# Slots by rank of token count: 576 or 600 per expert, with weights loaded from register addresses

## The chip, the cores and the metric

The kernel runs on one core of a Trainium2 chip. A core has five engines with queues of their own: TensorE (PE in the profile, with its weight loads as PEld), VectorE (DVE), ScalarE (ACT), GpSimd (POOL), and SyncE (SP), which here mostly issues DMA transfers. The metric is device time in microseconds (us); lower is better. The profile is of one execution and names source lines as L123.

## The reference

Attention with a threshold is followed by a mixture of experts that routes every token by a hash of its id.

```python
# q, k, v: (8, 8, 576, 64) float32
scores = np.matmul(q, k.transpose(0, 1, 3, 2)) / np.sqrt(64)
thresh = np.max(scores, axis=-1, keepdims=True) - tau
scores = np.where(scores >= thresh, scores, -1e9)
attn = np.exp(scores - np.max(scores, axis=-1, keepdims=True))
attn = attn / (np.sum(attn, axis=-1, keepdims=True) + 1e-09)
x = np.matmul(attn, v)      # laid out as (4608 tokens, 512)
expert_idx = token_ids * np.int64(2654435761) % np.int64(8)
for e in range(8):          # w1: (8, 512, 1024), w2: (8, 1024, 512)
    mask = expert_idx == e
    out[mask] = np.maximum(x[mask] @ w1[e], 0.0) @ w2[e]
```

All data is float32. The seed of the inputs is fixed, so the number of tokens of each expert is known: 598, 596, 571, 565, 599, 533, 570 and 576 for experts 0 to 7.

## The kernel before

**Attention** takes about 455 us and loops over 32 pairs of heads. A pair `p` has `NS = 5` steps `n`: one with the last 64 queries of both heads and four with 128 queries. `score` (L222) forms scores on TensorE, `negate` (L233) moves them from PSUM with their row extreme on VectorE, `expo` (L247) is the exponential on ScalarE. GpSimd forms the threshold `thr` (L240), and `mask` (L258) on VectorE multiplies weights by the threshold test and sums them. `turn_w` transposes on TensorE (L269), `put_wT` copies (L290), `av_part` multiplies by v (L300), and `put_xm` (L339) normalises and stores 128 columns of the attention result to the DRAM tensor `x_scratch` (L345, L350). The order of everything is written out by hand in the loop over `n` (L656 to L751) and each queue keeps it. In step `n`, masks belong to step `n - 1` and transposes to step `n - 2`. SP loads pairs two ahead. GpSimd also scales k (`scale_k`, L202).

**Routing** is a generator, `route()` (L353). Each `next(pieces)` issues a few small operations on `[128, 8]`, `[128, 36]` or `[128, 288]` elements, up to the next `yield`. It is called at two steps of a pair (L670 and L721) until `placed`. The route counts tokens per expert, finds each token's rank in its expert and then its slot. The slots of expert `e` are a region of `SL = 608`, laid out as 32 columns of 19; the first 24 columns take 19 tokens and the last eight take 18, which makes `CAP = 600`. Tokens past `CAP` go to overflow tiles of 128 slots. Then `scatters()` (L492) writes token numbers to slot tables in DRAM (`slot_scratch`), one indirect DMA of GpSimd per step, and SP reads the tables back (L506, L510) as indices for gathers and scatters of rows.

**The move to the experts.** `load_w1` and `load_w2` for experts 0 and 1 are issued on SP in pairs 20, 22, 24 and 26. From pair 26 on GpSimd gathers columns of `x_scratch` for expert 0 (`fetch_0`, L119, L113). `early_xT` transposes them, and `early_h` (L587) does three quarters of expert 0's first layer ahead of the last gather. `late_h` (L604) adds the last quarter.

**Experts** go in the order 0 to 7, one at a time, from about 490 us. Both layers use a scheme of seven products on half matrices (`seven`, L846) instead of eight. The two halves of the token dimension have `CH = CAP // 2 = 300` columns; the matmuls are at L859. VectorE forms sums of half matrices (L791, L794), ScalarE copies and applies the relu (L869, L866). The last expert's second layer works on two halves of 240 (`CHL`), and a separate last tile (L908) does the rest. `put_out` (L915) transposes output rows on TensorE (L927), copies them (L937, L939) and scatters them to their places with GpSimd (L943). `turn_x` (L959) transposes the next expert's rows on VectorE and moves quarters by SP's DMA (L971). During expert `e`, SP loads the weights of `e + 2`. A loop over overflow tiles follows; the number of its turns is read to registers by `values_load` at L1039. With the counts above it has none.

Each weight load names its expert when the program is built:

```python
def load_w1(e):
    w1_sb = w_pool.tile([P, CO, F], FP32, name="w1_sb")
    nc.sync.dma_start(out=w1_sb[:], in_=w1[e].rearrange("(c p) f -> p c f", p=P))
```

## Time and profile before

| | |
|---|---|
| time, median of 3 runs | 948.47 us (948.05 to 948.58) |
| profiled execution, its own time | 950.67 us |
| its span, first to last instruction | 949.0 us |
| TensorE busy, share | 933.1 us, 98% |
| VectorE busy, share | 734.1 us, 77% |
| ScalarE busy, share | 478.1 us, 50% |
| GpSimd busy, share | 306.1 us, 32% |
| granted TensorE clock | 0.998 |

Busy shares are averages over two stages with different limits. Matmul ends are modelled, so the distance between starts says more than the length of one. A float32 matmul appears as two records. In a row of the timeline, "x16" is the number of instructions merged, and a bracket at the end gives the idle time before the row and what ended it. In a table of windows, each engine has its busy time and in parentheses the number of its instructions; then come the granted clock, the share of the DMA engines' time and GB/s. In groups by line, the numbers after the bar are busy time, mean ns of one, and idle time before. Rows with three times (as 477/477/477) give the shortest, median and longest duration in ns.

### The profile page before, as it was taken

The numbers are of one execution on the slowest core, as the hardware profiler recorded it, in microseconds if no ns is written. First come the engines' busy times: TensorE is split into PE (matmuls) and PEld (weight loads), VectorE is DVE, ScalarE is ACT, GpSimd is POOL, SyncE is SP. The second block draws the span as 40 slices with busy tenths as digits, with TensorE's granted clock in tenths as the row PEclk, the third lists the DMA queues.
The fourth block names the chain that finished last, engine by engine and source line by source line (L and its number), as shares of the span: only waits on it lengthen the run. The fifth ranks groups of instructions, "written<-read, shape, count | busy, mean of one in ns | idle before, by whom it ended". The sixth has DMA issues, their size and how long they took to land.

```text
span 949.0 us, 21042 instructions
## 1 busy us (share of the span) xinstructions
PE 933.1 (98%) x7779; PEld 645.1 (68%) x7779; DVE 734.1 (77%) x1638; ACT 478.1 (50%) x778; POOL 306.1 (32%) x413
## 2 busy tenths in 40 slices
PE   8999999999999999999999999999999999999996
PEld 5666666666666666666677777777777777777785
DVE  7999999999999999999457755756557566575541
ACT  6988888888898888888320211202112021120310
POOL 4233233237767633565034310403003030110202
PEclk9999999999999999999999999999999999999999
DMA  7355456446447866841017435254442445311101
GB/s 174 90 142 133 106 133 144 104 125 138 103 91 213 204 164 143 202 107 39 26 31 216 159 93 175 89 156 158 109 158 89 142 159 140 139 46 34 50 1 51
DMA packets 113511, 113.31 MB, mean 119 GB/s; under 512 B 31183, under 2 KB 88015, under 8 KB 113409
## 3 DMA queue, kind: packets, MB, share of 16 engines
q1 hardware_dynamic: 105168, 92.84, 36.5%
q0 software_dynamic: 7808, 18.91, 6.6%
q8 instruction: 63, 1.03, 0.5%
q14 instruction: 40, 0.32, 0.1%
q10 hardware_dynamic: 432, 0.21, 0.1%
HBM read 81.99 MB, written 21.72 MB: 109 GB/s over the span
## 4 chain that ended last, share of the span: by engine, by line
PE 58%; issue 31%; DVE 5%; POOL 2%; DMA 2%; ACT 1%; SPq 0%; POOLq 0%; DVEq 0%; ACTq 0%
PE av L300 16%; PE sc L222 14%; PE bank L859 13%; PE tr L269 10%; PE sc L587 3%; DVE w L258 2%; PE av L269 1%; DVE ns L233 1%; POOL out_dram L943 1%; DMA out_dram<-o_sb,gidx 1%; DVE xq L963 1%; ACT w L247 1%; POOL xg L113 1%; PE xT_ps L604 0%; PE sc L604 0%
## 5 line engine op out<-in xcount | busy, mean ns | idle before, releaser
L247 ACT ACTIVATE w<-ns,nmx 128x576 f32<-128x576 f32 x288 | 220.4, 776 | 34.9 <-DVE ns L233 34.7
L258 DVE SCALAR_TENSOR_TENSOR w<-ns,thr,w 128x576 f32<-128x576 f32 x288 | 226.0, 816 | 1.3 <-POOL thr L240 1.3
L233 DVE TENSOR_SCALAR_CACHE_REDUCE ns<-sc 128x576 f32<-128x576 f32 x288 | 205.2, 744 | 3.9 <-PE sc L222 3.1
L222 PE MATMUL sc<-k_sb,q 64*128 64x288 f32 (+1 forms) x1280 | 179.8, 426 | 0.8 <-DVE ns L233 0.4
L269 PEld LDWEIGHTS tr<-ident,w 64*128 64x128 f32 x2624 | 106.4, 138 | 88.0 <-ACT wT_b L290 26.0
L240 POOL TENSOR_SCALAR thr<-nmx,drop 128x2 f32<-128x2 f32 (+1 forms) x160 | 103.2, 645 | 182.9 <-DVE ns L233 172.2
L943 POOL DMA_INDIRECT out_dram<-o_sb,gidx x39 | 47.6, 1220 | 292.4 <-ACT o_sb L939 277.5
L269 PE MATMUL tr<-ident,w 64*128 64x64 f32 x2624 | 138.7, 230 | 2.6 <-ACT wT_a L290 2.0
L869 ACT COPY p<-bank 128x600 f32<-128x600 f32 (+1 forms) x22 | 14.4, 654 | 201.4 <-PE bank L859 200.6
L222 PEld LDWEIGHTS sc<-k_sb,q 64*128 64x128 f32 (+1 forms) x1280 | 93.0, 179 | 24.0 <-DVE ns L233 10.6
L300 PE MATMUL av<-wT_a,v 128*64 128x320 f32 (+1 forms) x704 | 100.4, 418 | 0.0
L866 ACT ACTIVATE h<-h 128x600 f32<-128x600 f32 x56 | 39.4, 703 | 119.5 <-DVE h L794 119.0
L859 PE MATMUL bank<-h,w_sb 128*128 128x300 f32 (+1 forms) x384 | 97.3, 410 | 0.9 <-DVE h L609 0.9
L290 ACT COPY wT_a<-tr 128x512 f32<-128x512 f32 (+1 forms) x128 | 81.7, 638 | 19.8 <-PE tr L269 19.5
L859 PE MATMUL bank<-xT,w_sb 128*128 128x300 f32 x336 | 89.4, 416 | 0.0
L859 PEld LDWEIGHTS bank<-h,w_sb 128*128 128x128 f32 x384 | 72.9, 190 | 22.9 <-DVE h L609 1.3
L290 ACT COPY wT_b<-tr 128x512 f32<-128x512 f32 (+1 forms) x128 | 81.2, 635 | 5.0 <-PE tr L269 2.6
L300 PE MATMUL av<-wT_b,v 128*64 128x256 f32 x640 | 83.2, 389 | 0.0
L859 PEld LDWEIGHTS bank<-xT,w_sb 128*128 128x128 f32 x336 | 63.8, 190 | 21.0
L859 PE MATMUL bank<-h_s,w_s 128*128 128x300 f32 (+1 forms) x256 | 64.3, 410 | 0.0
L300 PEld LDWEIGHTS av<-wT_a,v 128*64 128x64 f32 x704 | 43.7, 136 | 28.6
L859 PE MATMUL bank<-x_s,w_s 128*128 128x300 f32 x224 | 59.6, 419 | 0.0
(147 smaller groups left out, 1106.7 us busy)
## 6 DMA issues: line engine op xcount, KB each, us to landing
w_sb<-in_moe_w_dram SPq DMA_DIRECT2D x16, 2048.0 KB
q<-in_q_dram SPq DMA_DIRECT2D x62, 288.0 KB
v<-in_v_dram SPq DMA_DIRECT2D x32, 256.0 KB
x_scratch<-xm SPq DMA_DIRECT2D x32, 256.0 KB
xT<-xq SPq DMA_DIRECT2D x84, 80.0 KB
k_sb<-in_k_dram SPq DMA_DIRECT2D x31, 144.0 KB
k_sb<-in_k_dram SPq DMA_DIRECT2D x32, 112.0 KB
x_scratch<-xg SPq DMA_DIRECT2D x9, 256.0 KB
```

Of the source, the lines that this page charges most:

```text
L222: nc.tensor.matmul(sc[out_rows, i, 0:S2], lhsT=q_sb[rows, h, q0:q1], rhs=k_sb[rows, h], start=True, stop=True)
L233: nc.vector.tensor_scalar(out=ns[:].rearrange("p (i s) -> p i s", i=2), in0=sc[:, :, 0:S2], scalar1=-1.0, scalar2=None, op0=ALU.mult, op1= ...
L240: nc.gpsimd.tensor_scalar(out=thr[:, 0:j + 1], in0=stats[n][0][:, 0:j + 1], scalar1=drop[:], scalar2=None, op0=ALU.add)
L247: nc.scalar.activation(w, nss[n, j][:], AF.Exp, bias=stats[n][0][:, j:j + 1], scale=-1.0)
L258: nc.vector.scalar_tensor_tensor(out=w, in0=nss.pop((n, j))[:], scalar=stats[n][1][:, j:j + 1], in1=w, op0=ALU.is_le, op1=ALU.mult, accum_ ...
L269: nc.tensor.transpose(dst[:, r, 64 * c:64 * c + 64], src[rows, c0:c0 + P], ident[rows, rows])
L290: nc.scalar.copy(dst, tr[:, :, 0:64 * n_c].rearrange("p r (c q) -> p r c q", c=n_c))
L300: nc.tensor.matmul(av[64 * j:64 * j + 64, g, c0:c1], lhsT=v_sb[:, c, 64 * j:64 * j + 64], rhs=wT[g][:, i, c0:c1], start=(c == 0), stop=stop)
L587: nc.tensor.matmul(h_ps[:, i, 0:CH], lhsT=w1_sb[:, co, fo * P:fo * P + P], rhs=xT_0[:, co, i * CH:i * CH + CH], start=(co == 0), stop=(co ...
L859: nc.tensor.matmul(ps[:, i, 0:width], lhsT=x[:, c, c0:c0 + P], rhs=y[:, c], start=c == 0, stop=c == n_k - 1)
L866: nc.scalar.activation(c, c, AF.Relu)
L943: inst = nc.gpsimd.indirect_dma_start(out=out[:, :], out_offset=bass.IndirectOffsetOnAxis(ap=idx, axis=0), in_=o_sb, in_offset=None, bound ...
```

## The change

Experts are taken in the order of their token counts. The route compares a key, count times 8 plus the expert's number, among all experts: `pos` is an expert's place in the order and `order` its inverse. Places 0 to 4 have `LOW = 576` slots (32 columns of 18), places 5 to 7 have 600 as before. Regions still start every 608 slots, now by place and not by expert. The rank is packed with the place (from bit 19) and the first overflow tile (six bits from bit 13). Several steps of the route go from VectorE to GpSimd. Three more calls of the route are added, at step 2 of pairs 9, 11 and 13.

`order_i` holds the order as integers. Each of the 16 weight loads on SP first reads its expert from there to a register (`expert_at`) and takes the DRAM address from it. All half widths of an expert in places 0 to 4 become 288, and its fifth tile of output rows has 64 rows, not 88. The expert in the last place keeps its 240-column halves.

```diff
@@ -59,14 +59,20 @@
+    N_LOW = 5
+    LOW = SL - 32
+    caps = [LOW] * N_LOW + [CAP] * (E - N_LOW)
...
-    TROWS = [P] * (KT - 1) + [CAP - FIRST[-1]]
-    CH = CAP // 2
...
+    def t_rows(e, kt):
+        return min(P, caps[e] - FIRST[kt])
...
-    assert all((N - (m - 1) * (CAP + 1) - CAP + P - 1) // P + m - 1 <= NOV
-               for m in range(1, E + 1) if m * (CAP + 1) <= N)
+    assert all((N - (m - 1) * (LOW + 1) - LOW + P - 1) // P + m - 1 <= NOV
+               for m in range(1, E + 1) if m * (LOW + 1) <= N)
+    assert all((r * 3641) >> 16 == r // (NB - 1) for r in range(N))
@@ -118,14 +125,21 @@
+    def expert_at(e):
+        return nc.values_load(order_i[0:1, e:e + 1], engines=[mybir.EngineType.SP],
+                              min_val=0, max_val=E - 1)
...
-        nc.sync.dma_start(out=w1_sb[:], in_=w1[e].rearrange("(c p) f -> p c f", p=P))
+        nc.sync.dma_start(out=w1_sb[:],
+                          in_=w1[bass.ds(expert_at(e), 1)].rearrange("o (c p) f -> p (o c) f", p=P))
...
-        nc.sync.dma_start(out=w2_sb[:], in_=w2[e].rearrange("(c p) d -> p c d", p=P))
+        nc.sync.dma_start(out=w2_sb[:],
+                          in_=w2[bass.ds(expert_at(e), 1)].rearrange("o (c p) d -> p (o c) d", p=P))
@@ -414,7 +435,27 @@
-            nc.vector.tensor_scalar(out=ot_i[:], in0=cnt[:, E:2 * E], scalar1=float(P - 1 - CAP),
+            nc.vector.scalar_tensor_tensor(out=key[:], in0=cnt[:, E:2 * E], scalar=float(E),
+                                           in1=iota_f[:, 0:E], op0=ALU.mult, op1=ALU.add)
+            nc.vector.tensor_tensor(out=pairs[:], in0=key[:, None, :].to_broadcast([P, E, E]),
+                                    in1=key[:, :, None].to_broadcast([P, E, E]), op=ALU.is_lt)
+            yield
+            nc.vector.reduce_sum(pos[:], pairs[:], axis=AX.X)
+            nc.gpsimd.tensor_scalar(out=big_e[:], in0=pos[:], scalar1=float(N_LOW),
+                                    scalar2=None, op0=ALU.is_ge)
+            nc.vector.tensor_tensor(out=pairs[:], in0=pos[:, None, :].to_broadcast([P, E, E]),
+                                    in1=iota_f[:, 0:E, None].to_broadcast([P, E, E]),
+                                    op=ALU.is_equal)
+            nc.gpsimd.tensor_tensor(out=pairs[:], in0=pairs[:],
+                                    in1=iota_f[:, None, 0:E].to_broadcast([P, E, E]),
+                                    op=ALU.mult)
+            yield
+            nc.vector.scalar_tensor_tensor(out=key[:], in0=big_e[:], scalar=float(LOW - CAP),
+                                           in1=cnt[:, E:2 * E], op0=ALU.mult, op1=ALU.add)
+            nc.vector.reduce_sum(order[:], pairs[:], axis=AX.X)
+            nc.gpsimd.tensor_copy(order_i[:], order[:])
+            yield
+            nc.vector.tensor_scalar(out=ot_i[:], in0=key[:], scalar1=float(P - 1 - LOW),
@@ -429,6 +470,8 @@
+            nc.vector.scalar_tensor_tensor(out=base[:], in0=pos[:], scalar=float(1 << 19),
+                                           in1=base[:], op0=ALU.mult, op1=ALU.add)
@@ -443,29 +486,40 @@
-            nc.vector.tensor_scalar(out=rank_i[:, 2], in0=rank_i[:, 0], scalar1=13, scalar2=None,
+            nc.vector.tensor_scalar(out=rank_i[:, 2], in0=rank_i[:, 0], scalar1=13, scalar2=63,
+                                    op0=ALU.logical_shift_right, op1=ALU.bitwise_and)
+            nc.vector.tensor_scalar(out=rank_i[:, 3], in0=rank_i[:, 0], scalar1=19, scalar2=None,
...
-            yield
-            nc.vector.tensor_copy(rank[:], rank_i[:, 1])
-            nc.vector.tensor_scalar(out=rank_f[:], in0=rank[:], scalar1=float(-1 - FULL), scalar2=0.0,
+            nc.gpsimd.tensor_copy(rank[:], rank_i[:, 1])
+            nc.gpsimd.tensor_copy(place[:], rank_i[:, 3])
+            nc.gpsimd.tensor_scalar(out=big[:], in0=place[:], scalar1=float(N_LOW),
+                                    scalar2=None, op0=ALU.is_ge)
+            nc.gpsimd.tensor_copy(ovt[:], rank_i[:, 2])
+            yield
+            nc.vector.scalar_tensor_tensor(out=rank_f[:], in0=big[:], scalar=float(-FULL),
+                                           in1=rank[:], op0=ALU.mult, op1=ALU.add)
+            nc.gpsimd.tensor_scalar(out=rank_f[:], in0=rank_f[:], scalar1=-1.0, scalar2=0.0,
...
-            yield
-            nc.vector.tensor_copy(ovt[:], rank_i[:, 2])
-            nc.vector.tensor_scalar(out=rank_i[:, 0], in0=rank_f[:], scalar1=57.0, scalar2=None,
+            nc.gpsimd.tensor_scalar(out=ovt[:], in0=ovt[:], scalar1=float(P),
+                                    scalar2=float(E * SL - LOW), op0=ALU.mult, op1=ALU.add)
+            yield
+            nc.vector.tensor_scalar(out=rank_i[:, 0], in0=rank_f[:], scalar1=3641.0, scalar2=None,
...
-            nc.vector.tensor_scalar(out=rank_i[:, 0], in0=rank_i[:, 0], scalar1=10, scalar2=None,
+            nc.vector.tensor_scalar(out=rank_i[:, 0], in0=rank_i[:, 0], scalar1=16, scalar2=None,
...
-            nc.vector.tensor_scalar(out=ovt[:], in0=ovt[:], scalar1=float(P),
-                                    scalar2=float(E * SL - CAP), op0=ALU.mult, op1=ALU.add)
-            nc.vector.scalar_tensor_tensor(out=first[:], in0=eidf[:], scalar=float(SL),
+            nc.vector.scalar_tensor_tensor(out=first[:], in0=place[:], scalar=float(SL),
...
-            yield
-            nc.vector.tensor_tensor(out=ovt[:], in0=ovt[:], in1=first[:], op=ALU.subtract)
-            nc.vector.scalar_tensor_tensor(out=ovt[:], in0=rank[:], scalar=float(CAP),
+            nc.vector.scalar_tensor_tensor(out=rank_f[:], in0=big[:], scalar=float(LOW - CAP),
+                                           in1=rank[:], op0=ALU.mult, op1=ALU.add)
+            nc.vector.scalar_tensor_tensor(out=ovt[:], in0=big[:], scalar=float(LOW - CAP),
+                                           in1=ovt[:], op0=ALU.mult, op1=ALU.add)
+            yield
+            nc.gpsimd.tensor_tensor(out=ovt[:], in0=ovt[:], in1=first[:], op=ALU.subtract)
+            yield
+            nc.vector.scalar_tensor_tensor(out=ovt[:], in0=rank_f[:], scalar=float(LOW),
...
-            yield
-            nc.vector.tensor_tensor(out=first[:], in0=first[:], in1=rank[:], op=ALU.add)
+            nc.gpsimd.tensor_tensor(out=first[:], in0=first[:], in1=rank[:], op=ALU.add)
@@ -584,15 +642,16 @@
-                        nc.tensor.matmul(h_ps[:, i, 0:CH], lhsT=w1_sb[:, co, fo * P:fo * P + P],
-                                         rhs=xT_0[:, co, i * CH:i * CH + CH],
+                        nc.tensor.matmul(h_ps[:, i, 0:CH0], lhsT=w1_sb[:, co, fo * P:fo * P + P],
+                                         rhs=xT_0[:, co, i * CH0:i * CH0 + CH0],
...
-                                h_0[:, fo].rearrange("p (i t) -> p i t", i=2), h_ps[:, :, 0:CH])
+                                h_0[:, fo, 0:caps[0]].rearrange("p (i t) -> p i t", i=2),
+                                h_ps[:, :, 0:CH0])
@@ -667,7 +726,7 @@
-                if s == 3 and p > 0 and not placed:
+                if (s == 3 and p > 0 or s == 2 and p in (9, 11, 13)) and not placed:
@@ -810,8 +870,10 @@
-        def x_blocks(x):
-            return [x[:, C2 * j:C2 * j + C2, CH * k:CH * k + CH] for j in range(2) for k in range(2)]
+        def x_blocks(e):
+            x, half = xT_bufs[e % 2], caps[e] // 2
+            return [x[:, C2 * j:C2 * j + C2, half * k:half * k + half]
+                    for j in range(2) for k in range(2)]
@@ -821,7 +883,7 @@
-            return CH if e < E - 1 else CHL
+            return caps[e] // 2 if e < E - 1 else CHL
```

The same widths replace `CH` and `TROWS` in the early and late parts of layer 1, in `sums_x`, `layer1`, `put_out` and `turn_x`.

## The prediction

> **What bounds the kernel now.** I read the busy totals and the forty slices first, then the table of windows, then the timelines of single engines where a window raised a question.
>
> ```profile
> PE 933.1 (98%) x7779; PEld 645.1 (68%) x7779; DVE 734.1 (77%) x1638; ACT 478.1 (50%) x778; POOL 306.1 (32%) x413
> ...
> DVE  7999999999999999999457755756557566575541
> ```
>
> A busy PE of 98% says little alone, because the ends of matmuls are modelled. The second line divides the kernel: VectorE is full for some 19 of 40 slices (attention, to about 455 us) and about six tenths busy after (experts). Two windows, one head pair of attention and one expert, give the bound of each stage. The columns are length, then PE, PEld, DVE, ACT and POOL busy time.
>
> ```profile
> 257.13:271.02 13.89, 13.89 (x178) 8.81 (x174) 13.84 (x39) 12.29 (x21) 9.92 (x13) 1.00 0.49 108
> ```
>
> ```profile
> 559.90:618.50 58.60, 58.35 (x265) 43.66 (x264) 36.91 (x47) 10.21 (x16) 11.17 (x10) 1.00 0.43 134
> ```
>
> A pair lasts 13.89 us and VectorE works 13.84 of them: attention is bound by VectorE, with TensorE close behind. An expert lasts 58.6 us, TensorE works 58.35, VectorE 36.91, ScalarE 10.21: the expert stage is bound by TensorE alone, and what is taken from its matmuls is taken from the end. Weight loads (PEld, 190 ns each) lie beneath the matmuls. In the PE timeline of the last two experts:
>
> ```profile
> 866.72 4.20 PE L859 MATMUL bank<-h_s,w_sb 128*128 128x300 f32 x16
> 870.75 4.20 PE L859 MATMUL bank<-h,w_sb 128*128 128x300 f32 x16
> ...
> 922.37 3.40 PE L859 MATMUL bank<-h_s,w_sb 128*128 128x240 f32 x16
> 925.61 3.40 PE L859 MATMUL bank<-h,w_sb 128*128 128x240 f32 x16
> ```
>
> From start to start, 16 records of 300 columns take 4.03 us (252 ns each) and 16 of 240 columns take 3.24 us (202.5 ns). Sixty columns are worth 49 to 50 ns, so the price is 0.83 ns a column with no fixed part to be seen, and 288 columns, between the two, should cost 10.0 ns less than 300.
>
> **Part 1, narrower matmuls (gain).** Experts in places 0 to 4 go from two halves of 300 to two of 288. Each layer of an expert has 112 records (7 products x 2 x 4 matmuls in the second layer, each seen as two records). Place 0 has 96 early and 32 late records of layer 1 and 112 of layer 2, which is 240. Places 1 to 4 have 224 each, 896. In sum 1136 x 10.0 ns = **11.4 us**. Places 5 to 7 keep 300, and the last layer keeps its 240. The early records hide the last gathers: these are issued from 475.38 to 482.67 us, land 2.5 to 3.0 us after their start for the last two, so by about 485, and TensorE comes to their transposes at 486.99. With 64 early records behind the last `xm`, 0.64 us of this 2 us cover goes, and none is paid. VectorE and ScalarE get shorter too (24 elements of a 600-element add), under TensorE and worth nothing. The counts (533, 565, 570, 571, 576 and 596, 598, 599) fit 576 and 600, so the overflow loop stays at zero turns in both kernels.
>
> **Part 2, an old wait grows (loss).** In layer 1 TensorE reaches a bank that ScalarE has yet to empty, since its output buffers wait on the row scatters.
>
> ```profile
> 595.75 2.29 PE L859 MATMUL bank<-x_s,w_sb 128*128 128x300 f32 x8 [0.25 <-ACT o_sb L939]
> ```
>
> Between the output transposes and this wait lie 16 records; at 288 they end 0.16 us sooner while the scatters don't. Over places 1 to 4 that is 4 x 0.16 = **0.6 us** given back. If ScalarE and the scatters were fast enough, zero.
>
> **Part 3, more routing (loss).** The routing sits in the VectorE-bound stage. The starts of `xm` (L339) show pairs of 13.89 us without routing and up to 14.31 with it; the sum of the excess over pairs 1 to 12 is 2.1 us, for operations whose own times sum to 6.75 us. So about 0.31 of the nominal time reaches the end. The nearest rows:
>
> ```profile
> L433 DVE TENSOR_TENSOR incl<-incl,base 128x288 f32<-128x288 f32 x1 | 0.5, 450 | 0.0
> ...
> L465 DVE SCALAR_TENSOR_TENSOR ovt<-rank,ovt 128x36 f32<-128x36 f32 x1 | 0.2, 195 | 0.0
> ```
>
> VectorE gains four operations on 64 elements (about 0.21 us each, between these rows), three on 8 elements (0.16) and four on 36 (0.18): 2.06 us. Six on 36 elements leave for GpSimd (L449, L450, L453, L459, L464, L468: 1.08 us). Net 0.98 us, of which 0.31 is 0.3 us. Bounds: all of it, 1.0 us, and a gain of 0.3 if the six leaving ones were the exposed ones (the two pairs with L449 to L461 have excess 0.42 and 0.27).
>
> GpSimd gets eleven operations. Small ones take 0.22 to 0.29 us (L330). What queues behind them is `thr` (L240), for which `mask` on VectorE waits; but `thr` of a step is used a step later, about 3 us after the issue, and a piece has four at most. So in-order waiting costs nothing; without that cover each would add about 0.3 us. The Trainium skill speaks against it, though (SBUF — State Buffer, Who interferes with whom): a VectorE instruction with two SBUF inputs and a GpSimd one that reads SBUF exclude each other, the later waiting for the whole of the earlier. The row for `mask`, which has two SBUF inputs:
>
> ```profile
> L258 DVE SCALAR_TENSOR_TENSOR w<-ns,thr,w x288: 799/810/1274, 10.0 to 455.5; 128x576 f32<-128x576 f32 x144
> ```
>
> By the rule alone VectorE could lose up to eleven small operations, 11 x 0.29 = 3.2 us. The row says that the loser is nearly always GpSimd: the median is 810 ns beside a minimum of 799, though the 0.75 us `scale_k` (L202) runs in each pair and `thr` (mean 0.71 us for two columns, 0.29 at best) bears the lock. I take 0.3 us, by the row; the rule would make the forecast 2.9 us later. Part 3: **0.6 us**, from -0.3 to 4.2.
>
> The three extra calls of the route (pairs 9, 11, 13) offset three added stops, so `placed` still falls in pair 14, and the scatters keep their place.
>
> **Part 4, register addresses (loss).** Each of 16 weight loads is preceded on SP by a register load. The row is the one at L1039:
>
> ```profile
> L1039 SPq TENSOR_LOAD <-ov_i x1: 477/477/477, 475.6 to 475.6; - x1
> L1039 SPq FUSED_REGOPS  x1: 192/192/192, 476.2 to 476.2; - x1
> ```
>
> With the assert (37 ns) and one more register operation for the address it is T = 0.9 us. The skill's nearest price is about 1.3 us for several registers read from HBM (Runtime: NRT & Kernel Launch, The ~15µs preamble/postamble breakdown); this is one from SBUF, so I stay with the row. In the expert stage SP issues w1 at 626.10 for use near 680, and w2 at 640.48 for use near 704: some 50 us of cover hides T, and a transfer of up to that length. In attention two of the four loads are exposed. SP runs behind from w1 of place 1 until after w2 of place 1, and the stores of `x` and the gathers follow in a chain:
>
> ```profile
> 345.56 0.59 SPq L123 DMA_DIRECT2D w_sb<-in_moe_w_dram  x1
> ...
> 376.51 0.59 SPq L128 DMA_DIRECT2D w_sb<-in_moe_w_dram  x1
> ...
> 393.74 0.38 SPq L345 DMA_DIRECT2D x_scratch<-xm  x1
> ```
>
> The gather at 397.43 waits for that store, `thr` at 398.58 stands behind the gather, and VectorE stops:
>
> ```profile
> 398.92 0.82 DVE L258 SCALAR_TENSOR_TENSOR w<-ns,thr,w 128x576 f32<-128x576 f32 x1 [0.73 <-POOL thr L240]
> ```
>
> That pair takes 15.58 us instead of 13.89. A shift by T at each load reaches the gathers undiminished or partly: between 0 (SP's slack takes it) and 2T with T by the skill's figure and 0.23 us of register work, 3.1 us. I take **1.4 us**, between T and 2T.
>
> **Sum.** -11.4 + 0.6 + 0.6 + 1.4 = -8.8 us. The profiled execution took 950.67 us around a span of 949.0; its like after would be 941.9 with a span of 940.2. The three timed runs have a median 2.2 us below it; taking the 8.8 from that median gives **939.7 us**.
>
> **Rivals.**
> (a) Attention takes half of it back: the chain at pairs 26 and 27 at 3.1 us and the lock at 3.2, with 0.98 us of routing work fully exposed. -11.4 + 0.6 + 4.2 + 3.1 = -3.5, **945.0 us**. For it: VectorE has 0.05 us free in a pair. Against: the routing of today passes only a third, and no `mask` row shows a systematic loss.
> (b) Slower: a load from a register address moves its 2 MB more slowly. The place is w2 of place 1, which ran from 376.51 until SP's wait for it ended at 388.8 (12.3 us); the gathers issued in that time landed after 8.0 us, and the store at 393.74 waited for them, so each further microsecond goes to the end. From 8.8 us longer it is slower than before, from 10.7 measurably; at twice the time, 939.7 + 12.3 = **952.0 us**. For it: no such load is in this trace. Against: shape and contiguous rows stay, and all SP loads already sit in a queue of the dynamic kind.
> (c) 288 columns bring no more than 300 (a granule in the matmul), parts 3 and 4 stay and part 2 falls away: 948.47 + 2.0 = **950.5**. Against it stands the 240-column row on the same line.
>
> **How the numbers follow.** Likeliest 0.70, with an own range of 937.1 (no cost at all) to 942.5; (a) 0.21; (b) 0.06; (c) 0.03. The range takes the likeliest and most of (a): 937.0 to 944.5. A change under 0.2% (1.9 us) can't be told from none: faster 0.90, same 0.02 (the far end of a), slower 0.08.
>
> **What the next profile must show.** Windows of about 56.4 us for four experts and 58.6 for the later ones; start to start 3.88 us for 16 records of 288; 96 early records in 0.96 us less; waits of TensorE for `o_sb` near 0.4 to 0.6; pairs 9 to 13 at no more than 14.4 us; a register load near 0.5 us ahead of each weight load; pair 27 near 16 to 17 us. It is wrong if attention ends over 5 us later, if an expert of 576 slots gains under 1.5 us, or if TensorE waits for a weight tile.

## The result, and the profile after

| | before | after |
|---|---|---|
| time, median | 948.32 us (948.05 to 948.58) | **937.98 us** (937.65 to 938.14) |
| ratio to before, interval | | 0.989 (0.987 to 0.991) |
| profiled execution, its own time | 950.67 us | 938.01 us |
| its span | 949.0 us | 936.4 us |

The runs of before in the table are those made beside the runs of after. The kernel is 10.3 us faster in the medians; the forecast was 8.8 us. The two profiles lie 12.7 us apart, and 2.2 us of that belong to the profiled execution of before, as the forecast had assumed. A second profile of the same kernel, taken later (first experiment), has a span of 947.1 us, and below it is this one that stands for before.

Line numbers have moved: the `mask` is now L272, `xm` L353, the matmuls of both layers L921, `thr` L254. The page first: busy times, and VectorE in forty slices.

```profile
PE 919.9 (98%) x7775; PEld 643.1 (69%) x7775; DVE 731.2 (78%) x1643; ACT 476.4 (51%) x776; POOL 308.6 (33%) x424
...
DVE  8999999999999999999457665756667566675541
```

TensorE lost 13.2 us of work and kept its share; the two stages and their bounds are where they were. The table of windows, one expert of 576 slots and one of 600 (length, then PE, PEld, DVE, ACT, POOL):

```profile
552.25:609.13 56.88, 56.15 (x266) 43.67 (x265) 36.06 (x47) 10.00 (x16) 10.95 (x11) 1.00 0.45 137
749.34:807.99 58.65, 58.39 (x265) 43.67 (x264) 36.92 (x46) 10.21 (x16) 11.09 (x10) 1.00 0.43 135
```

The narrow expert is 1.8 us shorter and TensorE is still the bound. Of its 56.88 us TensorE is idle for 0.73, against 0.26 in the wide one. The timeline of TensorE in the narrow expert shows both the gain and this idle time:

```profile
567.77 4.04 PE L921 MATMUL bank<-h_s,w_sb 128*128 128x288 f32 x16
571.65 4.04 PE L921 MATMUL bank<-h,w_sb 128*128 128x288 f32 x16
...
589.62 2.21 PE L921 MATMUL bank<-x_s,w_sb 128*128 128x288 f32 x8 [0.73 <-ACT o_sb L1001]
```

From 567.77 to 571.65 sixteen records took 3.88 us, 242.5 ns each: 10.0 ns less than at 300 columns. The wait for `o_sb`, in its bracket, is the old wait that the forecast let grow.

Attention tells the rest. The starts of `xm` mark the pairs (us, from one start to the next; the number is that of the later `xm`, counted from 0):

| stretch | before, second profile | after |
|---|---|---|
| first `xm` | 32.58 | 32.93 |
| pairs 1 to 13, the routing | 182.67 | 184.31 |
| pairs 14 to 26 | 181.03 | 180.78 |
| pair 27 | 14.77 | 14.04 |
| pairs 28 to 30 | 41.11 | 41.45 |
| pair 31 | 16.91 | 15.73 |
| last `xm` to the end of the span | 478.03 | 467.16 |

Three of these were not foreseen as they are: routing costs more (+1.6), pair 27 is not longer but shorter, and pair 31 gains 1.2 us.

### The profile page after: what moved, and what is told of

The parts are those of the page before. It is cut to its first block, busy times and chain, and to the rows that moved or that the text cites. A ratio compares the mean times of both kernels' runs of the same rounds, so it can differ in the third digit from the quotient of the medians.

```text
span 936.4 us, 21124 instructions
## 1 busy us (share of the span) xinstructions
PE 919.9 (98%) x7775; PEld 643.1 (69%) x7775; DVE 731.2 (78%) x1643; ACT 476.4 (51%) x776; POOL 308.6 (33%) x424
## 4 chain that ended last, share of the span: by engine, by line
PE 61%; issue 29%; DVE 3%; ACT 2%; POOL 2%; DMA 2%; POOLq 0%; SPq 0%; DVEq 0%; ACTq 0%
PE av L314 18%; PE sc L236 15%; PE bank L921 12%; PE tr L283 11%; PE sc L645 3%; PE av L283 1%; POOL out_dram L1005 1%; DMA out_dram<-o_sb,gidx 1%; ACT w L261 1%; DVE xq L1025 1%; DVE h L854 1%; POOL xg L120 1%; DVE ns L247 0%; PE xT_ps L663 0%; PE sc L663 0%
## 5 line engine op out<-in xcount | busy, mean ns | idle before, releaser
L272 DVE SCALAR_TENSOR_TENSOR w<-ns,thr,w 128x576 f32<-128x576 f32 x288 | 226.4, 818 | 0.0
L254 POOL TENSOR_SCALAR thr<-nmx,drop 128x2 f32<-128x2 f32 (+1 forms) x160 | 105.0, 656 | 180.9 <-DVE ns L247 168.9
L931 ACT COPY p<-bank 128x576 f32<-128x576 f32 (+2 forms) x22 | 14.1, 642 | 195.3 <-PE bank L921 195.0
L236 PEld LDWEIGHTS sc<-k_sb,q 64*128 64x128 f32 (+1 forms) x1280 | 92.0, 177 | 24.0 <-DVE ns L247 10.7
L928 ACT ACTIVATE h<-h 128x576 f32<-128x576 f32 (+1 forms) x56 | 38.8, 692 | 117.5 <-DVE h L854 117.3
L921 PE MATMUL bank<-h,w_sb 128*128 128x288 f32 (+2 forms) x384 | 94.9, 404 | 0.8 <-DVE h L668 0.8
L921 PE MATMUL bank<-xT,w_sb 128*128 128x288 f32 (+1 forms) x336 | 87.5, 410 | 0.0
L921 PEld LDWEIGHTS bank<-h,w_sb 128*128 128x128 f32 x384 | 72.9, 190 | 20.5 <-DVE h L668 1.3
L921 PEld LDWEIGHTS bank<-xT,w_sb 128*128 128x128 f32 x336 | 63.8, 190 | 19.1
L921 PE MATMUL bank<-h_s,w_s 128*128 128x288 f32 (+2 forms) x256 | 62.7, 404 | 0.0
L120 POOL DMA_INDIRECT xg<-x_scratch,gidx_x x35 | 36.4, 1041 | 68.7 <-DVE xq L1025 52.5
```

The source lines that it names most:

```text
L120: nc.gpsimd.indirect_dma_start(out=dst, out_offset=None, in_=src, in_offset=bass.IndirectOffsetOnAxis(ap=idx, axis=0), bounds_check=src.sh ...
L236: nc.tensor.matmul(sc[out_rows, i, 0:S2], lhsT=q_sb[rows, h, q0:q1], rhs=k_sb[rows, h], start=True, stop=True)
L254: nc.gpsimd.tensor_scalar(out=thr[:, 0:j + 1], in0=stats[n][0][:, 0:j + 1], scalar1=drop[:], scalar2=None, op0=ALU.add)
L272: nc.vector.scalar_tensor_tensor(out=w, in0=nss.pop((n, j))[:], scalar=stats[n][1][:, j:j + 1], in1=w, op0=ALU.is_le, op1=ALU.mult, accum_ ...
L921: nc.tensor.matmul(ps[:, i, 0:width], lhsT=x[:, c, c0:c0 + P], rhs=y[:, c], start=c == 0, stop=c == n_k - 1)
L928: nc.scalar.activation(c, c, AF.Relu)
```

## The experiments

Each kernel is shown as an edit to the changed kernel, unless it says otherwise. Four of them ran in each of three series; each series had its own chip and its own runs of before as yardstick (medians 948.55, 955.24 and 958.37 us). Totals are compared inside a series. The first series has no run of the changed kernel, but its before lies within 0.25 us of the one in the table (948.32), so the table's 937.98 stands beside it. In the second series, without the changed kernel, only stretches of the profile are compared with that kernel.

### The kernel before, once more

No edit. The question was whether the stop of VectorE in pair 27 (a pair of 15.58 us in the first profile of before) belongs to that kernel (so that the register loads would stand behind it) or to one execution.

> The kernel before, unchanged, for a second profile. In the profiles of before and after, the stop of VectorE in pair 27 (pair of 15.58 us) is gone after the change (14.04 us), though the prediction had it grow by 1.4 us. Theory A: the stop belongs to that one execution of before; this profile then has pair 27 at 13.9 to 14.4 us and a span near 946.7 us. Theory B: the kernel before always has the stop and the change removed it; this profile has it again, at 15.3 us or more, and a span near 949 us.

Measured: 948.81 us, span 947.1 us, pair 27 14.77 us, between the two expectations. The timeline of VectorE:

```profile
400.51 0.82 DVE L258 SCALAR_TENSOR_TENSOR w<-ns,thr,w 128x576 f32<-128x576 f32 x1 [0.58 <-POOL thr L240]
```

The stop is there again, at 0.58 us and not 0.73, in a pair that is 0.8 us shorter. Its size varies from one execution to the next, so a difference of a microsecond in pair 27 between two single profiles shows nothing.

### Without register loads

```diff
+    ORDER = (5, 3, 6, 2, 7, 1, 0, 4)
...
-                          in_=w1[bass.ds(expert_at(e), 1)].rearrange("o (c p) f -> p (o c) f", p=P))
+                          in_=w1[ORDER[e]].rearrange("(c p) f -> p c f", p=P))
...
-                          in_=w2[bass.ds(expert_at(e), 1)].rearrange("o (c p) d -> p (o c) d", p=P))
+                          in_=w2[ORDER[e]].rearrange("(c p) d -> p c d", p=P))
```

The order is written into the program and nothing else changes. The forecast's part 4 says that this gets 1.4 us back; the rival is that SP's slack takes the loads and nothing comes back.

> The changed kernel with the order of the experts written into the program (5, 3, 6, 2, 7, 1, 0, 4) for the weight loads: no register loads on SP, addresses fixed; the route stays. Step under test is the register term, predicted at 1.4 us. Theory of the prediction (register loads shift the gather chain of pairs 26 and 27): about 936.6 us, 1.4 less than the changed kernel. Rival (SP has slack for them): 937.7 to 938.2, no difference.

Measured: 938.58 us (937.37 to 939.48), span 936.4 us, the same as with register loads. From the `xm` of pair 13 to the last one it takes 251.92 us against 252.00. From there to the end of the span it takes 467.25 us against 467.18. The rival is right and **the term of 1.4 us is zero**, to about 0.1 us in both stretches. The register loads are there, and shorter than the forecast's 0.9 us. Their rows in the profile of after, in ns (shortest/median/longest):

```profile
L130 SPq TENSOR_LOAD <-order_i x16: 263/282/469, 111.3 to 790.6; - x16
L130 SPq FUSED_REGOPS  x16: 152/162/187, 111.8 to 790.9; - x16
L130 SPq SEQ_ASSERT  x16: 18/18/37, 112.1 to 791.1; - x16
```

With 42 and 38 ns for the address (L135) that is 0.54 us. SP's timeline around w2 of place 1, the load that the forecast had put on the chain of gathers, with registers:

```profile
374.99 1.15 SPq L364 DMA_DIRECT2D x_scratch<-xm  x2
377.02 0.39 SPq L141 DMA_DIRECT2D w_sb<-in_moe_w_dram  x1
```

and without:

```profile
375.44 1.19 SPq L366 DMA_DIRECT2D x_scratch<-xm  x2
376.67 0.59 SPq L143 DMA_DIRECT2D w_sb<-in_moe_w_dram  x1
```

With registers SP passes nothing on for 0.88 us after the store (376.14 to 377.02), without them for 0.04 us. Yet the weight load is issued only 0.35 us later, and the gathers behind it show nothing of that. The distance T of 0.9 us was right here, between two issues; that it adds up along the chain was wrong.

### All regions 600 slots wide

```diff
-    N_LOW = 5
+    N_LOW = 0
```

The whole machinery stays (places, register loads, GpSimd's operations), but every expert keeps 600 slots. This is the price without the gain: 2.0 us by the forecast's parts 3 and 4, with 10.8 us from here to the changed kernel.

> The changed kernel with no small places: all eight places have 600 slots, so all matmuls are as wide as before; the longer route, the order by count and the register addresses stay. It gives the price of the route and the addresses alone, and its distance to the changed kernel is the gain of the narrow matmuls. By the terms of the prediction: 948.3 + 0.6 + 1.4 = 950.3 us, and the changed kernel 10.8 less (11.4 less 0.6 of waits). By the pair lengths of the two profiles (pairs 5 to 12 are 1.65 us longer in sum, register loads cost nothing): 950.0 us, and 12.0 less. If the gain came from something else than narrow matmuls, it is below 945.

Measured: 950.23 us (949.86 to 951.51), ratio to before 1.0014 (1.0002 to 1.0026). The price is 1.7 us, close to what was forecast, but in another place: pairs 1 to 13 last 184.31 us, the same as in the changed kernel and 1.64 us more than before, while pair 27 lasts 13.89 us, with no stop. The way from here to the changed kernel is **12.3 us, not 10.8**. In the two spans (948.7 and 936.4) it lies as follows: 9.7 us from the first product of expert 0's second layer to the start of the first 600-slot expert (1008 records x 10.0 ns, less 0.42 for the waits for `o_sb`), 1.2 between the last `xm` and that product, and 1.17 in pair 31; the remaining 0.2 us are scattered. In pair 31 only some 24 records became narrower, 0.24 us; 0.93 us are something else. The 1.2 us hold about 104 narrower records, 1.04 us, and a little of something else too. The timeline of TensorE in pair 31, here:

```profile
456.82 1.18 PE L619 MATMUL sc<-ident,xg 64*128 64x64 f32 x6
457.93 0.52 PE L283 MATMUL tr<-ident,w 64*128 64x64 f32 x10
458.38 1.28 PE L645 MATMUL sc<-xT,w_sb 128*128 128x300 f32 x4
```

and in the changed kernel:

```profile
456.83 0.27 PE L619 MATMUL sc<-ident,xg 64*128 64x64 f32 x1
456.85 0.27 PE L283 MATMUL tr<-ident,w 64*128 64x64 f32 x1
456.94 0.22 PE L619 MATMUL sc<-ident,xg 64*128 64x64 f32 x1
456.96 0.26 PE L283 MATMUL tr<-ident,w 64*128 64x64 f32 x1
457.01 0.22 PE L619 MATMUL sc<-ident,xg 64*128 64x64 f32 x1
457.06 0.48 PE L283 MATMUL tr<-ident,w 64*128 64x64 f32 x8
457.47 1.24 PE L645 MATMUL sc<-xT,w_sb 128*128 128x288 f32 x4
```

These are the transposes of expert 0's fifth tile (L619). With 88 rows they are six, in chunks of 64 and 24 rows, and take 1.11 us from start to start; with 64 rows they are three, which run among the transposes of the weights. The records of layer 1 that follow (L645) start 0.91 us sooner. Uneven rows are what is dear, and not the change between two blocks of rows: the tiles ahead of the fifth one, each in chunks of 64 and 64 rows by turns, need far less. In pair 30 of the changed kernel, where these tiles are as in the wide one:

```profile
452.89 0.91 PE L619 MATMUL sc<-ident,xg 64*128 64x64 f32 x24
453.64 0.41 PE L283 MATMUL tr<-ident,w 64*128 64x64 f32 x8
```

These are 24 transposes in 0.75 us.

### The fifth tile with 88 rows again

```diff
+        def rows_88(kt):
+            return min(P, CAP - FIRST[kt])
...
-                    r1 = min(r + 64, t_rows(0, kt))
+                    r1 = min(r + 64, rows_88(kt))
...
-                    rows = t_rows(0, ka)
+                    rows = rows_88(ka)
```

Only the transposes of place 0's fifth tile, with their copies out of PSUM, go back to 88 rows; the matmuls stay at 288 columns. If those transposes were the 0.93 us, they come back; if the gain in pair 31 came from the narrower records, nothing does.

> The changed kernel, but the fifth tile of place 0 is transposed for the early layer 1 with 88 rows as before and not with 64; the 24 extra columns are used by nothing. The question is what shortens pair 31: it lasts 15.73 us after the change and 16.90 with eight wide places, and narrower matmuls explain 0.24 of the 1.17. Theory A (the 24-row transposes and their copies): pair 31 at 16.6 to 16.7 us and 1.0 us slower than the changed kernel, 939.0. Theory B (something else): pair 31 at 15.8 and no difference, 938.0.

Measured: 945.86 us (945.33 to 946.01), with before at 955.24. Pair 31 lasts 16.66 us, 0.93 more than the 15.73 of the changed kernel, and the timeline has the six transposes back:

```profile
463.45 1.18 PE L622 MATMUL sc<-ident,xg 64*128 64x64 f32 x6
464.56 0.52 PE L283 MATMUL tr<-ident,w 64*128 64x64 f32 x10
```

The gain in pair 31 is the fifth tile's, shown by the pair; the totals can't show it alone, since the changed kernel was not in this series. The way from the last `xm` to the first product of the second layer is 27.19 us here and 27.01 in the changed kernel: the last quarter of the same tile, transposed there, accounts for another 0.18 us.

### The route's GpSimd operations on VectorE

```diff
-            nc.gpsimd.tensor_scalar(out=big_e[:], in0=pos[:], scalar1=float(N_LOW),
+            nc.vector.tensor_scalar(out=big_e[:], in0=pos[:], scalar1=float(N_LOW),
```

So for all eleven. If GpSimd's operations lock VectorE out, as the rule that the forecast weighed says, this makes the route cheaper or leaves it; if they are free for VectorE, it makes it dearer.

> The changed kernel with the eleven GpSimd operations of the route on VectorE. Their sum on VectorE is about 2.0 us. Theory of the prediction (0.31 of the nominal time of the route reaches the end, GpSimd costs VectorE little): 0.3 to 0.6 us slower than the changed kernel, 938.4. Rival 1 (VectorE is full and every operation counts): 2.0 us slower, 940.0. Rival 2 (the lock between GpSimd and VectorE made the route's excess of 1.65 us): faster, about 937.

Measured: 938.71 us (938.3 to 939.52); pairs 1 to 13 last 185.61 us against 184.31, so eleven more operations on VectorE, some 2.0 us by their own length, cost 1.3 us. Pairs 28 to 30 get 0.33 us back (41.12 us, as before), and why is not settled. The rows of `mask`, first in the changed kernel, then here:

```profile
L272 DVE SCALAR_TENSOR_TENSOR w<-ns,thr,w 128x576 f32<-128x576 f32 x288 | 226.4, 818 | 0.0
```

```profile
L272 DVE SCALAR_TENSOR_TENSOR w<-ns,thr,w 128x576 f32<-128x576 f32 x288 | 225.8, 816 | 0.0
```

Were the lock at work on VectorE, the first should be longer by up to 3.2 us. It is 0.6 us longer, and the kernel with 600-slot regions, which has the same route on GpSimd, has 225.8 as well. So these eleven operations cost the masks nothing that can be told from the spread.

That is not because there is no lock. The trace of the changed kernel fits the rule on both sides, a mask that has begun before a GpSimd operation, and one that begins behind it:

```profile
196.13 0.82 DVE L272 SCALAR_TENSOR_TENSOR w<-ns,thr,w 128x576 f32<-128x576 f32 x1
196.34 0.73 POOL L518 TENSOR_TENSOR ovt<-ovt,first 128x36 f32<-128x36 f32 x1
...
220.41 0.75 POOL L216 TENSOR_SCALAR k_sb<-k_sb,k_scale 128x576 f32<-128x576 f32 x1
220.80 0.95 DVE L272 SCALAR_TENSOR_TENSOR w<-ns,thr,w 128x576 f32<-128x576 f32 x1
```

In the first two rows the operation of the route comes second and takes 0.73 us, where its like (`first`, L522) takes 0.26; the mask keeps its 0.82. In the last two `scale_k` comes first, and the mask takes 0.95 us. Such masks, over 0.9 us, number 12 of 288 in this trace and 11 and 10 in the two profiles of before, all from pair 14 on, behind the routing, and each begins with 0.3 us or more of `scale_k` still to run; the 17 masks of this trace that begin under its last 0.2 us keep their 0.81. The longer the rest, the longer the mask: with 0.34, 0.42 and 0.69 us of `scale_k` to run it takes 0.94, 1.02 and 1.29. The pairs with one of them show no loss: pairs 14 to 19 have one each and last 13.89 us like pair 23, which has none.

### All regions wide, experts in the old order

```diff
-    N_LOW = 5
+    N_LOW = 0
...
-            nc.vector.scalar_tensor_tensor(out=key[:], in0=cnt[:, E:2 * E], scalar=float(E),
+            nc.vector.scalar_tensor_tensor(out=key[:], in0=cnt[:, E:2 * E], scalar=0.0,
```

With the key reduced to the expert's number the order is 0 to 7 as before. It asked whether the stop in pair 27 comes from which expert's rows are gathered first.

> The kernel with eight places of 600 slots and the longer route, but the experts keep the order 0 to 7 (the key leaves the counts out). Place 0 is again an expert of 598 tokens, not of 533. The question is why VectorE's stop in pair 27 (pair of 15.58 and 14.77 us in two profiles of before) is 13.88 to 14.04 us in all four profiles with the new route. Theory A (its early gathers fetch fewer rows, 533 for 598): the stop is back, pair 27 at 14.7 us or more. Theory B (the new route moves the phase of the gathers, or the stop is chance): pair 27 at 13.9 to 14.1 us.

Measured: 956.45 us in one execution, pair 27 14.85 us. This doesn't decide: in this series pair 27 lasts 14.41 to 14.85 us in all four kernels, those that gather the smallest expert first among them.

### No routing at step 0

```diff
             nc.vector.tensor_copy(row[:], incl[:, :, NTC - 1])
             yield
-            yield
...
                              stop=True)
+            yield
             nc.vector.tensor_copy(cnt[:], tr[:, 0:2 * E])
...
-                if (s == 3 and p > 0 or s == 2 and p in (9, 11, 13)) and not placed:
+                if (s in (2, 3) and p > 0 or s == 4 and p in (9, 11, 13)) and not placed:
...
-                if s == 0 and p > 0 and not placed:
-                    next(pieces)
```

The same operations, at other steps of the pair. Two timelines of VectorE had pointed here. In the kernel before (second profile) the two steps of `ot_i` stand at step 3, in the middle of a pair, and a single copy stands at step 0, right ahead of `xm`:

```profile
95.85 0.16 DVE L417 TENSOR_SCALAR ot_i<-cnt 128x8 int32<-128x8 f32 x1
96.05 0.17 DVE L419 TENSOR_SCALAR ot_i<-ot_i 128x8 int32<-128x8 int32 x1
...
102.72 0.17 DVE L422 CAST ot<-ot_i 128x8 f32<-128x8 int32 x1
102.80 0.82 DVE L339 TENSOR_TENSOR xm<-av,rec 128x640 f32<-128x640 f32 x1
```

In the changed kernel the route has three pieces more ahead of these, an odd number, and so what stood at step 3 has moved to step 0:

```profile
117.42 0.17 DVE L458 TENSOR_SCALAR ot_i<-key 128x8 int32<-128x8 f32 x1
117.62 0.17 DVE L460 TENSOR_SCALAR ot_i<-ot_i 128x8 int32<-128x8 int32 x1
117.83 0.82 DVE L353 TENSOR_TENSOR xm<-av,rec 128x640 f32<-128x640 f32 x1
```

One operation delays `xm` by 0.08 us here (102.72 to 102.80), two that depend on each other by 0.41 (117.42 to 117.83). Three pairs in a row (5, 6 and 7, with `pos`, `ot_i` and `oend`) have such a couple at step 0, and they last 0.38, 0.34 and 0.38 us longer than before, 1.1 of the 1.64 us that the route has added.

> The changed kernel with the stops of the route moved from steps 0 and 3 of a pair to steps 2 and 3 (the three extra ones to step 4), and the counts' matmuls one stop ahead of their copy. The work is the same. In both profiles a stop at step 3 adds next to nothing up to 0.45 us of work, while stops at step 0 add 0.1 to 0.4 us each; the route's excess over pairs 1 to 12 is 3.7 us in the changed kernel. Theory A (steps 2 and 3 have slack, step 0 has none): excess of 1 to 2 us, 936 us. Theory B (VectorE is full anywhere, only the amount of work counts): 3.4 to 4.0 us of excess, 937.9.

Measured: 942.91 us (941.53 to 943.62), pairs 1 to 13 in **182.92 us against 184.31**. Of the route's added cost, 1.64 us, 1.39 are gone, though VectorE does the same operations. Two dependent ones in the new place, in the middle of the pair:

```profile
96.15 0.16 DVE L438 SCALAR_TENSOR_TENSOR key<-cnt,iota_f 128x8 f32<-128x8 f32 x1
96.34 0.22 DVE L440 TENSOR_TENSOR pairs<-key 128x64 f32<-128x64 f32 x1
```

This pair (the fifth) lasts 14.08 us, against 14.55 in the changed kernel. What an operation of the route costs depends on the step at which it stands, and not on its length alone. The middle of a pair is cheaper but not free: beyond 13.89 us a pair, the whole route costs 3.7 us in the changed kernel, 2.3 here and 2.1 in before, and pair 8, which takes five operations of the route at three steps here, lasts 14.49 us. The 2.3 us are above the 1 to 2 expected and well below the 3.4 of the other theory. Why the middle of a pair takes most of it without loss, on an engine that is nearly full, these runs don't show.

### A third size for the smallest expert

```diff
-    caps = [LOW] * N_LOW + [CAP] * (E - N_LOW)
+    TINY = SL - 64
+    caps = [TINY] + [LOW] * (N_LOW - 1) + [CAP] * (E - N_LOW)
```

The smallest expert has 533 tokens, so place 0 can have 544 slots: halves of 272 columns, 13.3 ns less for each of its 240 records, 3.2 us. The rest of the edit makes the slot arithmetic depend on the place: GpSimd gets ten more small operations, VectorE one fewer.

> The changed kernel with a third size: place 0 has 544 slots (32 columns of 17), places 1 to 4 have 576, places 5 to 7 have 600. The smallest expert has 533 tokens. The route gets nine more GpSimd operations; VectorE has the same number. Theory A (0.83 ns a column holds on down, and GpSimd work is free): 240 records x 16 columns x 0.83 ns = 3.2 us faster than the changed kernel, 934.8. Theory B (a floor under the narrow matmuls, or GpSimd's work held against the masks): less than 1.5 us faster, 936.5 or more.

Measured: 941.10 us (940.84 to 941.38), ratio to before 0.985 (0.983 to 0.987). Pairs 1 to 12 last 170.45 us (170.42 in the changed kernel) and don't feel the added operations on GpSimd. From pair 31 on the kernel is 2.3 us shorter than the changed one (pair 31 15.52 for 15.74 us, and from the last `xm` to the end 465.06 for 467.18), less than the 3.2 expected. Place 0's second layer gives the whole of its part, 1.5 us for 112 records. Place 1 gives part back: it has no wait for `o_sb` in the changed kernel, and one here.

```profile
536.24 2.21 PE L938 MATMUL bank<-x_s,w_sb 128*128 128x288 f32 x8 [0.41 <-ACT o_sb L1018]
```

The rest of the shortfall is not accounted for.

### The third series: before, after, and the moved route again

The first two kernels have no edit. The third is the kernel without routing at step 0.

> The kernel before once more, beside the changed kernel on one chip. On a second chip all kernels were some 6.7 us slower, in pairs 14 to 29, and there every profile had a pair 27 of 14.4 to 14.9 us, with and without small places, with the order by count and without. If the stop in pair 27 goes with the execution and the chip and not with the change, the pairs 26 and 27 of this profile and of the changed kernel's next one differ by no fixed sign; if the change removes it, the changed kernel's pair 27 is shorter by 0.7 us or more.

> The changed kernel again, on one chip with the two versions beside it. Expected 10.3 us under the kernel before on this chip, ratio 0.989.

> The changed kernel with the stops of the route at steps 2 and 3, on one chip with the changed kernel. Its profile of the other chip has pairs 1 to 13 shorter by 1.4 us (182.92 for 184.31). Theory A: 1.4 us faster than the changed kernel. Theory B (given back later, in the chain of the gathers): within 0.5 us.

Measured: before 956.85 us in this execution (median of the series 958.37), pair 27 14.56 us. After 945.99 us (943.72 to 947.07), ratio 0.987 (0.983 to 0.990), pair 27 15.91 us. The medians lie 12.4 us apart, not 10.3, but before ran here at granted clocks of 0.991 to 0.998. Its three runs at 0.997 or more (median 956.02) and the three of after at 0.997 (median 945.97) lie 10.1 apart, near the 10.3 of the table. In this series the changed kernel has the longer pair 27; in the first series before had it. There all kernels with the change lasted 13.9 to 14.0 us in it, and one could have booked the 0.7 us that before took longer as a gain of the change; this series has the opposite sign.

The moved route gave 947.06 us (943.32 to 948.26). Pairs 1 to 13 gain again, 182.89 us against 184.63 (0.36 of it in pair 13, where the scatters begin; pairs 1 to 12 gain 1.39, as before), but the total shows nothing: pairs 28 to 30 took 45.06 us against 43.60 in the same profiles, and the three runs of it above 946 us had a granted clock of 0.994, the one at 943.32 had 0.998. **For the total this is inconclusive**; the gain is shown for pairs 1 to 13 alone.

### Both together

```diff
-    caps = [LOW] * N_LOW + [CAP] * (E - N_LOW)
+    TINY = SL - 64
+    caps = [TINY] + [LOW] * (N_LOW - 1) + [CAP] * (E - N_LOW)
...
-                if (s == 3 and p > 0 or s == 2 and p in (9, 11, 13)) and not placed:
+                if (s in (2, 3) and p > 0 or s == 4 and p in (9, 11, 13)) and not placed:
...
-                if s == 0 and p > 0 and not placed:
-                    next(pieces)
```

with the two moved yields and the arithmetic of the 544-slot kernel.

> Both at once: a third size of 544 slots for place 0, and the stops of the route at steps 2 and 3. If the two gains add, it is 3.2 (240 records x 16 columns x 0.83 ns), less 0.4 for one more wait of TensorE for an output bank in place 1, plus 1.4 faster than the changed kernel: 4.2 us.

Measured: **940.24 us** (939.99 to 941.45), ratio to before 0.982 (0.979 to 0.985); its slowest run is 2.3 us below the fastest of the changed kernel in the same series, its median 5.8 us below. It beats the kernel before and the changed kernel. Expected were 4.2 us. The stretches that the two edits touch give 3.8 of the 5.8 in the two profiles: pairs 1 to 13 last 183.15 us for 184.63, and from pair 31 on 2.3 us are gained. The rest lies in pairs 14 to 30, whose lengths vary from one execution to the next. TensorE's timeline in place 0's second layer:

```profile
517.72 3.83 PE L936 MATMUL bank<-h,w_sb 128*128 128x272 f32 x16
521.38 3.83 PE L936 MATMUL bank<-h,w_s 128*128 128x272 f32 x16
```

3.66 us for sixteen records of 272 columns is 228.8 ns each, 0.4 ns off the line through 202.5 at 240, 242.5 at 288 and 252.5 at 300.

## Why the prediction was right, and where it was wrong

The direction and the size were right. The first term, which outweighs all others, was exact. Two of the four terms were mis-sized in opposite directions (part 3 by 1.0 us too little, part 4 by 1.4 too much) and one gain was not seen. That the sum came within 1.5 us is in part luck.

| step | predicted, us | measured, us | from |
|---|---|---|---|
| part 1: 1136 narrower records | -11.4 | -11.4 | 10.0 ns each, starts in the timeline |
| fifth tile with 64 rows | not in the sum | -0.9 | wide and 88-row kernels, pair 31 |
| part 2: wait for `o_sb` | +0.6 | +0.4 | brackets in the timeline |
| part 3: routing | +0.6 | +1.6 | pairs 1 to 13 |
| part 4: register loads | +1.4 | 0 | kernel without them |
| sum | -8.8 | -10.3 | both medians; the rows above give the same |

That the rows meet the medians so closely is luck too: the two spans (947.1 and 936.4) lie 10.7 us apart, and outside these rows stand the first `xm` (+0.35), pairs 14 to 26 (-0.25), pair 27 (-0.73), pairs 28 to 30 (+0.34) and some -0.1 after the last `xm`.

**Part 1** held in mechanism and size. Rival (c), a granule in the matmul, is out: 272 and 288 columns lie on the line between 240 and 300. The same four figures are 0.833 ns a column and some 2.5 ns a record (2.1 at 272), so "no fixed part to be seen" was wrong by those 2.5 ns, which cancel in a difference. What the part left out are the other operations that 24 fewer slots touch. The forecast looked at the early records as cover for the gathers, and not at the transposes of expert 0's fifth tile, which stood in the same rows. Their count halves with 64 rows, and in pair 31 TensorE works 15.3 of 15.7 us, VectorE 3.9.

**Part 2** held with 0.14 us of growth at each of the waits in places 2 to 4 (0.73, 0.37 and 0.38 us, in the wide kernel 0.59, 0.23 and 0.24). Place 1 shows no such wait: three times 0.14, not four times 0.16. Against before, whose three waits are 0.26, 0.24 and 0.22 us, the one in place 2 has grown by more; but 0.33 us of that stand in the wide kernel too, so the narrower matmuls are not their cause, and what is stays open.

**Part 3** was mis-sized. The step that failed is "about 0.31 of the nominal time reaches the end", an average over all pieces of today's route applied to the added ones. By position the picture is another: the net added 0.98 us of VectorE's work cost 1.64, more than its own length, and the same operations off step 0 cost only 0.25 us over before (182.92 against 182.67). The upper bound of 1.0 us for work "fully exposed" was no bound, since three added pieces, an odd number, exchange step 0 and step 3 for the old pieces behind them. The trace of before could have said so: the pairs with a piece at step 3 alone (1, 2, 7 and 8, one operation of 0.45 us each) last 0.02 to 0.04 us longer there than 13.89, those with a piece at step 0 (3 to 6 and 9 to 12) 0.08 to 0.43, though they have a piece at step 3 as well, all but pair 4. The lock of GpSimd, the other half of part 3 and of rival (a), cost the masks nothing measurable through these operations; having them on GpSimd is worth 1.3 us in pairs 1 to 13. But "no `mask` row shows a systematic loss", the reason given against rival (a), is not so: the trace of before has 11 masks of 0.94 us or more, all behind the routing. That pairs 28 to 30 lengthen by 0.34 us was not foreseen; it is one wait of VectorE ahead of the `xm` of pair 30, and why it is longer is open.

**Part 4** failed at its second step. Its first step, T = 0.9 us, is what lies between two issues (0.88 us), though the instructions themselves take 0.54. "A shift by T at each load reaches the gathers undiminished or partly", between T and 2T, was wrong: the lower bound, SP's slack, was the answer. The forecast read pair 27 of one profile as the end of a chain at its limit. Pair 27 has since lasted 13.9 to 15.9 us, with a sign that differs between the series, and without register loads as with them (13.96 and 14.04 us). **What sets it is open**; what the runs exclude is that the register loads do. Rival (b), slower transfers from register addresses, falls with the same run: TensorE waits for no weight tile in the experts, and the span is the same without register addresses.

Of the signs that the forecast named, these held: 3.88 us for sixteen records, no wait for a weight tile, attention ending on time. These did not: the narrow expert shown lasts 56.88 us, not 56.4, with a wait of 0.73; pair 10 lasts 14.53 us, over 14.4; a register load takes 0.28 us, not 0.5 (0.54 with its check and the address); and pair 27 lasts 14.04 us, not 16 to 17.

## What to carry to other kernels

Price an operation added to a full engine by the place in its order where it will stand, and not by an average share of what passes through: here the same small operations cost 1.6 us over before, or 0.25. When sizes shrink, look for every loop whose trip count or chunking depends on them, beside the large matmuls; six transposes of uneven rows that became three were worth as much as 90 narrower matmul records. And before a stop in one profile is taken for a chain at its limit, see it in a second execution.

## What the runs showed of the hardware

A register load from SBUF on SP takes 0.28 us (0.26 to 0.47), with its check and the address 0.54 us. The issue of a DMA from such an address (medians 0.39 us for w1 and 0.37 for w2) is no slower than from a fixed one (0.54 and 0.37). A float32 matmul record shows no step at 240, 272, 288 and 300 columns: 0.83 ns a column and some 2.5 ns. Six transposes of alternately 64 and 24 rows took 1.11 us, three of 64 rows some 0.2 us, interleaved with others: far from a factor of two. Uneven ones start 0.20 and 0.17 us apart, even ones of alternate blocks 0.03; what makes them so dear was not tried. In the trace of after, a mask of VectorE that begins with 0.3 us or more of GpSimd's `scale_k` still to run takes 0.94 to 1.29 us (12 of them) and not 0.81, and `thr` of GpSimd takes 0.73 us in the mean where it begins under a mask (133 times) and 0.30 where it doesn't (27).

The kernel before took 948.55, 955.24 and 958.37 us in the three series. Between the profiles of the first and the third the difference arises almost only from pair 14 to the end of attention, where GpSimd issues scatters and gathers: pairs 14 to 21 took 111.17 and 116.46 us, pairs 1 to 13 182.67 and 182.68. Why is open; chip and time changed together.
